# Small TensorE products as 64- and 32-wide array tiles in an HGRN2 attention and low-rank mixer kernel

## The chip, the cores and the metric

The kernel runs on one core of one Trainium2 chip. The core's engines each work through their own instruction stream: TensorE (PE, with its weight loads listed as PEld), VectorE (DVE), ScalarE (ACT), GpSimd (POOL) and SyncE (SP, which issues DMAs). The metric is the device time of one execution in microseconds; the smaller the better. All operands are 32-bit floats.

## The reference, cut to what matters

Two blocks follow each other. The first is a gated linear recurrence over 768 steps for 4 batches of 8 heads of width 48; the second a mixer over the 768 positions (rank 32) and the 384 channels.

```python
# attention: q, k, v, f_logit are (4, 8, 768, 48)
f = sigmoid(f_logit)
for t in range(S):
    state = f[:, :, t, :, None] * state + k[:, :, t] (x) v[:, :, t]   # 48 x 48 per head
    y[:, :, t] = q[:, :, t] @ state
x = y as (4, 768, 8 * 48)
# mixer: U (768, 32), V (32, 768), w_ch1 (384, 1536), w_ch2 (1536, 384)
h = x.transpose(0, 2, 1) @ U @ V
u = x + h.transpose(0, 2, 1)
out = u + relu(u @ w_ch1) @ w_ch2
```

## The kernel before, in words

**Units.** A unit is a pair of heads of one batch; there are 16, four for each batch. The two heads (`par` 0 and 1) lie on partitions 0 to 47 and 64 to 111 of the transposed tiles (`PAD` is 64), and the 768 steps are cut into `NCH` = 6 chunks of `C` = 128. `prepare(n)` makes what unit n needs: VectorE turns f, k and q (`turned`, L237), ScalarE takes the sigmoid (L255), VectorE scans the gates from the back and from the front (L261, L280), and GpSimd multiplies k and q by the scans (L276, L285). `keep` also makes `whole`, the product of the gates of each chunk.

**`attend(n)`** has five pieces. `scores(0)` and `scores(1)` multiply k and q of each head and chunk (L308, `sc`; 48 rows, at partition 0 or 64) and VectorE masks the result into `A` (L315). `kept` transposes five chunks of k, both heads at once, on TensorE (L325, `pt`), and ScalarE copies them to `kb` (L329). `states` multiplies `kb` with v for both heads at once (L334, `ds`, 128 x 96), so that half of every product belongs to the wrong head; VectorE masks that half away with `own` (L339, `dn`), GpSimd scales by `whole` (L345, `st`), and four VectorE steps carry the state from chunk to chunk (L349). `read` adds, chunk by chunk, q times the state before the chunk (L359) and `A` times v for each head (L362) into `y`, and ScalarE copies y into `x` (L367).

**The mixer** of a batch is a list of pieces (`mixer_pieces`): `low_rank` (L73, `ph`: six products of 128 rows and 32 columns of U into one sum of 32 partitions, copied to `h` at L76), `mix` (L80, `pu`: 32 rows of V and h; VectorE adds to x at L81), `turn` (L89, `put`: transposes, ScalarE copy L91), `ch1` (L96, `pz`, ReLU at L99) and `ch2` (L105, `po`, add at L108, then the DMA out).

**Order.** The loop at L388 runs the pieces of `attend(n)`, puts the pieces of `prepare(n + 1)` between them, and after each calls `fill`, which takes pieces from the list `todo`. While batch 0's units run, `todo` holds the weight loads (L24: each weight is a 64-bit float in memory, DMA into `w_raw`, six VectorE steps L46 to L53, two GpSimd steps L54 and L55); while later units run, it holds the mixer of the batch before. The mixer of batch 3 runs alone at the end. Each engine's order within that is set by the tile framework's scheduler, which is why pieces interleave. PSUM has three double-bank tiles for sc, pt and y (`ps_big`) and two single-bank tiles for all else (`ps_mm`).

A TensorE product of 32-bit floats is seen in the trace as two MATMUL records, each with its own LDWEIGHTS record; a transpose is seen as one.

Of the kernel before, what the change touches and what calls it, by code (L numbers as in the profile page):

```python
# [16 lines left out]
WP = 384  # L17
# [6 lines left out]
def weight_loader(nc, pool, one, dma):  # L24
# [7 lines left out]
    def load(dst, w):  # L32
        if w.dtype == F32:
            dma.dma_start(out=dst, in_=w)
            return
        rows, cols = dst.shape
        raw = pool.tile([P, WP], U64, name="w_raw")
        dma.dma_start(out=raw[0:rows, 0:cols], in_=w)
# [21 lines left out]
def mixer_pieces(nc, b, x, U, V, w1, w2, ident, out, two, three, zp, ps_mm):  # L60
# [3 lines left out]
    R, FF = U.shape[2], w1.shape[2]  # L64
    NDC, NFC = DM // P, FF // P
# [4 lines left out]
    def low_rank():  # L70
        pm = ps_mm.tile([P, 512], F32, name="ph", tag="mm")
        for c in range(NCH):
            nc.tensor.matmul(pm[0:R, 0:DM], lhsT=U[:, c, :], rhs=x[:, c, :],  # L73
                             start=(c == 0), stop=(c == NCH - 1))
        h[0] = two.tile([R, DM], F32, name="h")
        nc.scalar.copy(h[0], pm[0:R, 0:DM])  # L76
# [46 lines left out]
def factored_path(ctx, tc, q, k, v, f_logit, moe_U, moe_V, moe_w_ch1, moe_w_ch2, out, ok):  # L123
# [20 lines left out]
    PW = 2 * D  # L144

    assert S % (2 * C) == 0 and H % 2 == 0 and NB < D <= PAD and PAD == 2 * NB and S % NB == 0
    assert DM % P == 0 and FF % P == 0 and FF % WP == 0 and DM == WP and DM <= 512 and R <= P
    assert G * PW <= 512 and G * C <= 512 and (NCH - 1) * PW <= 512

# [50 lines left out]

    own = const.tile([P, PW], F32, name="own")
    nc.vector.memset(own, 0.0)
    for par in range(2):
        for lo, n in ((0, NB), (NB, D - NB)):
            nc.vector.memset(own[par * PAD + lo : par * PAD + lo + n, par * D : (par + 1) * D], 1.0)
# [13 lines left out]
    V = const.tile([R, S], F32, name="V")  # L219
    load = weight_loader(nc, two, one, nc.sync)  # L220
    weights = [lambda c=c: load(U[:, c, :], moe_U[c * P : (c + 1) * P, :]) for c in range(NCH)]
    weights += [lambda o=o: load(V[:, o : o + WP], moe_V[:, o : o + WP]) for o in range(0, S, WP)]
# [70 lines left out]
    def attend(n):  # L293
# [28 lines left out]
        def kept():  # L322
            pt = ps_big.tile([P, 2, 512], F32, name="pt", tag="big")
            for c in range(NCH - 1):
                nc.tensor.transpose(pt[:, c // G, (c % G) * C : (c % G + 1) * C], T["k"][:, chunk[c]], ident)  # L325
            kb = T["kb"] = two.tile([P, NCH - 1, C], F32, name="kb")
            for a in range(2):
                lo, hi = a * G, min((a + 1) * G, NCH - 1)
                nc.scalar.copy(kb[:, lo:hi, :].rearrange("p c d -> p (c d)"), pt[:, a, 0 : (hi - lo) * C])  # L329

        def states():
            ds = ps_mm.tile([P, 512], F32, name="ds", tag="mm")
            for c in range(NCH - 1):
                nc.tensor.matmul(  # L334
                    ds[:, c * PW : (c + 1) * PW], lhsT=T["kb"][:, c, :],
# [406 lines left out]
```

## Time and profile before

| | |
|---|---|
| median of the runs | 722.86 us (lowest 721.62) |
| profiled execution | 721.53 us, of which 719.6 us span |
| PE busy | 614.4 us (85%), 2489 MATMUL records |
| PEld busy | 403.6 us (56%) |
| DVE busy | 336.6 us (47%) |
| POOL busy | 143.5 us (20%) |
| ACT busy | 98.1 us (14%) |
| mean granted TensorE clock | 0.913 |

Busy PE time is modelled from the records and is not useful work at full speed; a record's start is measured, so the distance from one start to the next is the better price. Idle time of an engine that nobody waits for costs nothing. The granted clock takes two values in this trace, 1.00 and 0.50 of full speed, and the mean over a stretch tells how much of it ran at the lower one.

### The profile page before, as it was taken

The numbers are of one execution on the slowest core, as the hardware profiler recorded it, in microseconds if no ns is written. First come the engines' busy times: TensorE is split into PE (matmuls) and PEld (weight loads), VectorE is DVE, ScalarE is ACT, GpSimd is POOL, SyncE is SP. The second block draws the span as 40 slices with busy tenths as digits, with TensorE's granted clock in tenths as the row PEclk, the third lists the DMA queues.
The fourth block names the chain that finished last, engine by engine and source line by source line (L and its number), as shares of the span: only waits on it lengthen the run. The fifth ranks groups of instructions, "written<-read, shape, count | busy, mean of one in ns | idle before, by whom it ended". The sixth has DMA issues, their size and how long they took to land.

```text
span 719.6 us, 6593 instructions
## 1 busy us (share of the span) xinstructions
PE 614.4 (85%) x2489; PEld 403.6 (56%) x2489; DVE 336.6 (47%) x539; ACT 98.1 (14%) x205; POOL 143.5 (20%) x123
## 2 busy tenths in 40 slices
PE   0776248297199999989999999999999999999996
PEld 0765244074176666547665766576656664555553
DVE  6668798999984566254553542354211201000000
ACT  1100001012021031011320120112201200220210
POOL 3123374656632220102111111012100000000000
PEclk9999999559589999975999999859999999799999
DMA  9801354533497320452202522100000000000000
GB/s 205 155 1 31 97 122 109 142 109 120 136 215 145 85 52 20 108 117 50 64 16 71 140 58 70 53 8 10 0 23 11 1 12 23 0 1 22 12 12 26
DMA packets 42176, 47.71 MB, mean 66 GB/s; under 512 B 29783, under 2 KB 32855, under 8 KB 42135
## 3 DMA queue, kind: packets, MB, share of 16 engines
q1 hardware_dynamic: 42134, 47.20, 27.2%
q8 instruction: 21, 0.34, 0.2%
q14 instruction: 21, 0.16, 0.1%
HBM read 42.47 MB, written 4.72 MB: 66 GB/s over the span
## 4 chain that ended last, share of the span: by engine, by line
PE 76%; DVE 14%; DMA 3%; issue 3%; POOL 2%; ACT 1%; SPq 1%; DVEq 0%; ACTq 0%; POOLq 0%
PE pz L96 25%; PE po L105 25%; PE sc L308 5%; PE y L362 5%; PE ds L334 4%; PE y L359 3%; PE pu L80 3%; PE ph L73 2%; DMA w_raw<-in_moe_w_ch_dram 2%; DVE kT L237 2%; PE put L89 2%; PE pt L325 2%; DVE w_m L48 2%; DVE X L261 1%; DVE fT L237 1%
## 5 line engine op out<-in xcount | busy, mean ns | idle before, releaser
L96 PE MATMUL pz<-uT,w 128*128 128x384 f32 x576 | 200.9, 502 | 0.0
L105 PE MATMUL po<-w,z 128*128 128x384 f32 x576 | 188.7, 487 | 0.0
L105 PEld LDWEIGHTS po<-w,z 128*128 128x128 f32 x576 | 108.7, 190 | 74.3
L96 PEld LDWEIGHTS pz<-uT,w 128*128 128x128 f32 x576 | 109.6, 196 | 71.2 <-issue 5.5
L308 PE MATMUL sc<-qT,kT 48*128 48x128 f32 x384 | 45.9, 370 | 86.9 <-POOL qT L285 86.9
L108 DVE TENSOR_TENSOR o<-x,po 128x384 f32<-128x384 f32 x24 | 13.3, 554 | 181.5 <-PE po L105 181.5
L308 PEld LDWEIGHTS sc<-qT,kT 48*128 48x128 f32 x384 | 35.5, 252 | 105.2 <-POOL qT L285 89.2
L99 ACT ACTIVATE z<-pz 128x384 f32<-128x384 f32 x96 | 47.1, 490 | 228.2 <-PE pz L96 228.2
L362 PE MATMUL y<-v_nat,A 128*128 128x48 f32 x384 | 70.7, 318 | 0.0
L362 PEld LDWEIGHTS y<-v_nat,A 128*128 128x128 f32 x384 | 69.2, 251 | 2.4
L276 POOL TENSOR_TENSOR kT<-kT,X 128x768 f32<-128x768 f32 x16 | 30.3, 1894 | 200.0 <-DVE kT L237 187.9
L315 DVE TENSOR_TENSOR A<-sc,causal 128x384 f32<-128x384 f32 x64 | 33.2, 551 | 63.6 <-PE sc L308 63.5
L359 PE MATMUL y<-st,qT 128*128 128x96 f32 x160 | 42.9, 359 | 4.8 <-POOL st L345 4.8
L237 DVE STREAM_TRANSPOSE qT<-q_raw 128x768 f32<-128x768 f32 x16 | 33.5, 2094 | 18.7 <-PE y L359 18.7
L285 POOL TENSOR_TENSOR qT<-qT,Y 128x768 f32<-128x768 f32 x16 | 29.4, 1839 | 63.2 <-DVE qT L237 62.8
L54 POOL TENSOR_SCALAR w_m<-w_m 128x384 f32<-128x384 f32 (+2 forms) x32 | 34.4, 1074 | 36.4 <-DVE w_m L48 23.4
L261 DVE TENSOR_TENSOR_SCAN X<-fz,ends 128x768 f32<-128x768 f32 x16 | 28.1, 1757 | 26.0 <-ACT fz L255 20.4
L345 POOL TENSOR_TENSOR st<-dn,whole 128x480 f32<-128x480 f32 x16 | 16.5, 1033 | 111.6 <-DVE dn L339 110.2
L359 PEld LDWEIGHTS y<-st,qT 128*128 128x128 f32 x160 | 32.7, 251 | 7.2 <-POOL st L345 5.9
L237 DVE STREAM_TRANSPOSE fT<-f_raw 128x768 f32<-128x768 f32 x16 | 33.3, 2079 | 6.4 <-DMA f_raw<-in_f_logit_dram 4.4
L237 DVE STREAM_TRANSPOSE kT<-k_raw 128x768 f32<-128x768 f32 x16 | 33.2, 2074 | 0.0
L80 PE MATMUL pu<-h,V 32*128 32x384 f32 x48 | 30.1, 731 | 3.1 <-ACT uT L91 1.7
(52 smaller groups left out, 424.0 us busy)
## 6 DMA issues: line engine op xcount, KB each, us to landing
w_raw<-in_moe_w_ch_dram SPq DMA_DIRECT2D x24, 384.0 KB, 3.6
f_raw<-in_f_logit_dram SPq DMA_DIRECT2D x63, 142.0 KB, 3.6
k_raw<-in_k_dram SPq DMA_DIRECT2D x63, 142.0 KB, 4.4
q_raw<-in_q_dram SPq DMA_DIRECT2D x63, 142.0 KB, 4.1
v_nat<-in_v_dram SPq DMA_DIRECT2D x32, 144.0 KB, 5.2
out_dram<-o SPq DMA_DIRECT2D x24, 192.0 KB, 1.9
w_raw<-in_moe_U_dram SPq DMA_DIRECT2D x6, 32.0 KB, 3.2
w_raw<-in_moe_V_dram SPq DMA_DIRECT2D x2, 96.0 KB
```

What stands on the lines that cost most here:

```text
L54: nc.gpsimd.tensor_scalar(m, m, 2.0**-20, None, ALU.mult)
L80: nc.tensor.matmul(pm[:, 0:DM], lhsT=V[:, t * P : (t + 1) * P], rhs=h[0], start=True, stop=True)
L96: nc.tensor.matmul(pm[:, 0:HALF], lhsT=w1[:, m, i * P : (i + 1) * P], rhs=uT[a][:, m, :], start=(m == 0), stop=(m == NDC - 1))
L99: nc.scalar.activation(z[a, i], pm[:, 0:HALF], AF.Relu)
L105: nc.tensor.matmul(pm[:, 0:DM], lhsT=z[a, i][:, s * P : (s + 1) * P], rhs=w2[:, i, :], start=(i == 0), stop=(i == NFC - 1))
L237: nc.vector.transpose(t.rearrange("p (i c) -> p c i", c=TB), bass.AP(src_tile.tensor, src_tile.offset, [list(src_tile.ap[0]), [D, TB], [1, ...
L261: nc.vector.tensor_tensor_scan(backwards(X, S - 1, S), backwards(f, S, S), backwards(ends, S - 1, S), 0.0, ALU.mult, ALU.add,)
L276: nc.gpsimd.tensor_tensor(kT, kT, T["X"], ALU.mult)
L308: nc.tensor.matmul(sc[:, par, c * C : (c + 1) * C], lhsT=T["k"][rows[par], chunk[g * G + c]], rhs=T["q"][rows[par], chunk[g * G + c]], sta ...
L315: nc.vector.tensor_tensor(T["A"][:, par, g * G : (g + 1) * G, :], sc[:, par, 0 : G * C].rearrange("p (c i) -> p c i", i=C), causal.unsquee ...
L359: nc.tensor.matmul(o, lhsT=T["q"][:, chunk[c]], rhs=T["st"][:, c - 1, :], start=True, stop=False, skip_group_check=True)
L362: nc.tensor.matmul(o[:, par * D : (par + 1) * D], lhsT=T["A"][:, par, c, :], rhs=vt[:, c, par, :], start=(c == 0), stop=True, skip_group_c ...
```

## The change

Small TensorE products get a smaller part of the array each, at different partitions, next to each other:

- **Score and state parts of y** (`read`). The 128 steps of a chunk are cut into two halves of 64 (`HC`), which land on PSUM partitions 0 to 63 and 64 to 127. The state part is now four products a chunk (48 rows, 64 columns, 48 wide: two heads by two halves), all 20 ahead of the score part; the score part is four products a chunk (128 rows, 64 columns, 48 wide), 24 in all. Each head has its own bank of `y`.
- **State updates** (`states`). Ten products of 128 rows, 64 columns, 48 wide, one per head, each on its own 64 partitions. The wrong-head half does not arise, so `own`, `dn` and the GpSimd step go: one VectorE step scales from PSUM into `st` (240 wide), and the four carry steps are 48 wide.
- **Transposes of k** (`kept`). Ten of 64 rows instead of five of 128, one bank per head; one ScalarE copy of 640 in place of two of 384 and 256.
- **U product** (`low_rank`). The six products go to four 32-column tiles (`NG` = 4), so that `h` is four partial sums on 128 partitions; V is loaded four times, one copy below the other, so that `mix` has 128 rows and adds the four sums up.

The lines of the changed kernel are shifted: `ph` L79, `pu` L86, `put` L95, `pz` L102, `po` L111, `pt` L327, `ds` L335, `st` L341 and L346, `y` L363 (state) and L372 (score).

```diff
     def load(dst, w, copies=1):
+        rows, cols = dst.shape
+        n = rows // copies
...
-        dma.dma_start(out=raw[0:rows, 0:cols], in_=w)
+        for i in range(copies):
+            dma.dma_start(out=raw[i * n : (i + 1) * n, 0:cols], in_=w)
...
         for c in range(NCH):
-            nc.tensor.matmul(pm[0:R, 0:DM], lhsT=U[:, c, :], rhs=x[:, c, :],
-                             start=(c == 0), stop=(c == NCH - 1))
-        h[0] = two.tile([R, DM], F32, name="h")
-        nc.scalar.copy(h[0], pm[0:R, 0:DM])
+            g = slice((c % NG) * R, (c % NG + 1) * R)
+            nc.tensor.matmul(pm[g, 0:DM], lhsT=U[:, c, :], rhs=x[:, c, :],
+                             start=(c < NG), stop=(c >= NCH - NG))
+        h[0] = two.tile([P, DM], F32, name="h")
+        nc.scalar.copy(h[0], pm[:, 0:DM])
...
-    V = const.tile([R, S], F32, name="V")
+    V = const.tile([P, S], F32, name="V")
...
             for c in range(NCH - 1):
-                nc.tensor.transpose(pt[:, c // G, (c % G) * C : (c % G + 1) * C], T["k"][:, chunk[c]], ident)
...
+                for par in range(2):
+                    r = slice(par * PAD, (par + 1) * PAD)
+                    nc.tensor.transpose(pt[:, par, c * PAD : (c + 1) * PAD], T["k"][r, chunk[c]], ident[r, r])
+            kb = T["kb"] = two.tile([P, 2, NCH - 1, PAD], F32, name="kb")
+            nc.scalar.copy(kb.rearrange("p h c d -> p h (c d)"), pt[:, :, 0 : (NCH - 1) * PAD])
...
-                nc.tensor.matmul(
-                    ds[:, c * PW : (c + 1) * PW], lhsT=T["kb"][:, c, :],
-                    rhs=vt[:, c].rearrange("p h d -> p (h d)"), start=True, stop=True,
-                )
-            dn = two.tile([P, NCH - 1, PW], F32, name="dn")
...
-            nc.gpsimd.tensor_tensor(
-                st, dn, T["whole"][:, 1:NCH].unsqueeze(2).broadcast_to((P, NCH - 1, PW)), ALU.mult
+                for par in range(2):
+                    nc.tensor.matmul(
+                        ds[par * PAD : (par + 1) * PAD, c * D : (c + 1) * D],
+                        lhsT=T["kb"][:, par, c, :], rhs=vt[:, c, par, :], start=True, stop=True,
+                    )
+            st = T["st"] = two.tile([P, NCH - 1, D], F32, name="st")
             nc.vector.tensor_tensor(
+                st, ds[:, 0 : (NCH - 1) * D].rearrange("p (c e) -> p c e", e=D),
+                T["whole"][:, 1:NCH].unsqueeze(2).broadcast_to((P, NCH - 1, D)), ALU.mult,
             )
...
+            for c in range(1, NCH):
+                for par in range(2):
+                    for a in range(2):
+                        nc.tensor.matmul(
+                            o(a, par, c),
+                            lhsT=T["q"][rows[par], c * C + a * HC : c * C + (a + 1) * HC],
+                            rhs=T["st"][rows[par], c - 1, :],
+                            start=(c == 1), stop=False, skip_group_check=True,
+                        )
             for c in range(NCH):
...
                 for par in range(2):
+                    for a in range(2):
+                        nc.tensor.matmul(
+                            o(a, par, c), lhsT=T["A"][:, par, c, halves[a]], rhs=vt[:, c, par, :],
+                            start=False, stop=True, skip_group_check=True,
+                        )
```

What stands on TensorE before, in a unit of batch 1 (`ds`, then `y`, with products of the mixer of batch 0 between them; x6 counts products):

```order
L96 MATMUL pz<-uT,w_127 128x384 x6
L334 MATMUL ds<-v_nat,kb 128x96 x5
L96 MATMUL pz<-uT,w_127 128x384 x3
L105 MATMUL po<-w_128,z 128x384 x12
L362 MATMUL y<-v_nat,A 128x48 x2
L359 MATMUL y<-st,qT 128x96
```

The last two rows go on in turn until `y` has five of L359 and six of L362. At the same place of the changed kernel:

```order
L102 MATMUL pz<-uT,w_121 128x384 x6
L335 MATMUL ds<-v_nat,kb 64x48 x10
L102 MATMUL pz<-uT,w_121 128x384 x3
L111 MATMUL po<-w_122,z 128x384 x12
L363 MATMUL y<-st,qT 64x48 x20
L372 MATMUL y<-v_nat,A 64x48 x24
L111 MATMUL po<-w_122,z 128x384 x24
```

The mixer's products stand where they stood; the 17 products of `y` have become 44, in two blocks, and the state part, which needs `st`, now comes first.

VectorE before, in the first units, from the masks of the scores to the next unit's gates:

```order
L315 TENSOR_TENSOR A<-sc,causal 128x384 x4
L339 TENSOR_TENSOR dn<-ds,own 128x480
L237 STREAM_TRANSPOSE fT<-f_raw_80 128x24x32
L349 SCALAR_TENSOR_TENSOR st<-st,whole 128x96 x3
L261 SCALAR_TENSOR_TENSOR X<-fz_118,ends 128x768
```

and in the changed kernel:

```order
L315 TENSOR_TENSOR A<-sc,causal 128x384 x4
L341 TENSOR_TENSOR st<-ds,whole 128x240
L346 SCALAR_TENSOR_TENSOR st<-st,whole 128x48 x2
L237 STREAM_TRANSPOSE fT<-f_raw_80 128x24x32
L346 SCALAR_TENSOR_TENSOR st<-st,whole 128x48 x2
```

Two of the carry steps now stand ahead of the next unit's turning of f, since they no longer wait for a GpSimd step; the turning of f still stands behind `ds`.

48 lines of the change are left out of this document (16 added, 32 removed).

## The prediction

> **What bounds the kernel now.** I read the page's first two parts, then the chain of waits by engine.
>
> ```profile
> span 719.6 us, 6593 instructions
> PE   0776248297199999989999999999999999999996
> DVE  6668798999984566254553542354211201000000
> PE 76%; DVE 14%; DMA 3%; issue 3%; POOL 2%; ACT 1%; SPq 1%; DVEq 0%; ACTq 0%; POOLq 0%
> ```
>
> Each digit is 18 us. PE has gaps in the first 11 slices (to about 204 us), where batch 0's units run and VectorE also unpacks the weights; from there on it is full. So two stages: a third in which VectorE and the hand-overs decide, and 515 us in which a microsecond of PE is a microsecond of time. I then took windows of that stage; the column PEclk is the granted clock.
>
> ```profile
> core 0: us, PE busy (x) PEld busy (x) DVE busy (x) ACT busy (x) POOL busy (x), PEclk, DMA share, GB/s
> 304.00:308.00 4.00, 4.00 (x23) 1.75 (x24) 3.51 (x4) 0.07 (x1) 0.00 (x0) 1.00 1.25 247
> 316.00:320.00 4.00, 4.00 (x14) 2.00 (x13) 0.95 (x2) 0.48 (x1) 0.00 (x0) 0.50 0.00 0
> 312.00:344.00 32.00, 30.51 (x107) 21.09 (x108) 14.08 (x20) 4.01 (x9) 4.57 (x3) 0.57 0.28 63
> 460.00:492.00 32.00, 32.00 (x120) 22.25 (x119) 15.86 (x24) 5.73 (x13) 4.56 (x3) 0.63 0.06 13
> 608.00:624.00 16.00, 15.73 (x42) 7.57 (x41) 3.10 (x6) 3.50 (x8) 0.00 (x0) 0.68 0.00 0
> ```
>
> Three stretches run partly at half clock, one per batch, each where the mixer's `pu` and `put` pieces stand: 32 x 0.43 / 0.5 = 27.5 us, 23.7 us and 10.2 us, together 61 us. PE is busy all through 316 to 320 and still gets half clock.
>
> Last, the timeline of TensorE for one unit at full clock: start, duration, line, records.
>
> ```profile
> 343.69 0.71 PE L325 MATMUL pt<-ident,kT 128*128 128x128 f32 x5
> 344.23 4.04 PE L96 MATMUL pz<-uT,w 128*128 128x384 f32 x12
> 348.20 0.94 PE L308 MATMUL sc<-qT,kT 48*128 48x128 f32 x12
> 349.07 4.14 PE L96 MATMUL pz<-uT,w 128*128 128x384 f32 x12
> 353.04 1.25 PE L334 MATMUL ds<-v_nat,kb 128*128 128x96 f32 x10
> 354.13 4.06 PE L96 MATMUL pz<-uT,w 128*128 128x384 f32 x12
> 358.03 0.54 PE L362 MATMUL y<-v_nat,A 128*128 128x48 f32 x4
> ...
> 361.76 4.10 PE L96 MATMUL pz<-uT,w 128*128 128x384 f32 x12
> ```
>
> Prices from start to start: `y` 361.76 - 358.03 = 3.73 us for 34 records, 0.110 each; `ds` 1.09 for 10, 0.109 each; `pt` 0.54 for 5. `y` and `ds` cost the same per record though one is mostly 48 and the other 96 wide, so not the width but the weight load of 128 columns sets the slot. `sc`, two heads on rows 0 and 64, does 12 records of the same 128 columns in 0.87, entry and exit included.
>
> **Part by part.** *The slot of a 64-column record.* The weight loads of U (32 columns) and of the mixer (128), both at full clock, and from the chain of waits a run of the mixer's products:
>
> ```profile
> L73 PEld LDWEIGHTS ph<-x,U 128*32 128x32 f32 x12 | 1.2, 109 | 3.2 <-issue 3.2
> L96 PEld LDWEIGHTS pz<-uT,w 128*128 128x128 f32 x7 | 1.3, 190 | 0.9
> ...
> 666.33 23.22 PE pz L96 x72
> ```
>
> 96 columns are 81 ns, 0.84 ns each; 64 columns make the slot 0.11 / 2 = 0.055 us. *Side by side.* If `sc`'s records took turns, 12 would be 1.3 us; 0.87 with entry and exit says that pairs run together: 6 slots of 0.11 are 0.66, which leaves 0.2 us beside the 0.1 us in which the last ones run out. The twelve pz records before `sc` take 0.322 each, as 23.22 / 72 says too, so they are done by 344.23 + 12 x 0.322 = 348.09, 0.11 before `sc`. I price a change between the whole array and a tiled form at 0.15 to 0.2 us.
>
> *y.* State part: 40 records on four tiles, at best 10 slots = 0.55, in pairs 20 = 1.1. Score part: 48 records on two column tiles, 24 slots = 1.32. Three changes of form, 0.5. That is 2.4 to 2.9 against 3.73; I take a gain of 1.1. Two tiles by columns are not seen in the trace: in turn, they would cost 48 slots = 2.64, and y 3.7 to 4.2. *ds.* 20 records in 10 slots 0.55 and two changes 0.35: a gain of 0.2; in turn 1.45, a loss of 0.36. *pt.* Ten records in five paired slots of half the width, 0.3, and two changes: 0.65 to 0.9, a loss of 0.1 to 0.35; I take 0.2, and 0.1 gained at ds. Per unit 1.1 + 0.1 - 0.2 = 1.0 us. In the full stage eight units (6, 7, 9 to 11, 13 to 15) lie outside the slow stretches: **-8 us**.
>
> *U product.* Twelve records one after the other now, in batch 1:
>
> ```profile
> 304.70 4.06 PE L73 MATMUL ph<-x,U 128*32 128x384 f32 x12
> 308.69 0.76 PE L325 MATMUL pt<-ident,kT 128*128 128x128 f32 x5
> ```
>
> 3.99 us, 0.33 a record. In four tiles two rounds of two records, 1.33 and 0.3 of changes: a gain of 2.35; in pairs of tiles 1.6. Batches 1 to 3, on PE's path each time: **-6 us** (5 to 7).
>
> *The clock.* In 304 to 308 stand U's products, 128 rows and 32 columns: clock 1.00. In 316 to 320 stand `pu` with 32 rows, `sc` with 48 and transposes: 0.50, with PE as busy. So rows in use seem to count. With V fourfold, `pu` has 128 rows. At best all 61 us run at full clock and take 30 us less, which also holds the units 8 and 12. But the first stretch begins with a real gap that the change leaves, and `pu` before and after:
>
> ```profile
> 313.49 0.65 PE L89 MATMUL put<-ident,x 128*128 128x128 f32 x3 [2.14 <-DVE x L81]
> 317.93 1.64 PE L80 MATMUL pu<-h,V 32*128 32x384 f32 x2
> 609.03 0.91 PE L80 MATMUL pu<-h,V 32*128 32x384 f32 x2
> ```
>
> (1.64 at half clock, 0.91 at full). At full clock the chain add, turn, copy would show: VectorE's 33 us in these 80 would sit in 50. I take half: **-16 us** (0 to -28).
>
> *The first 204 us.* Unit 1, VectorE with its idle time before, and the PE work it waits for:
>
> ```profile
> 40.18 1.66 PE L308 MATMUL sc<-qT,kT 48*128 48x128 f32 x12 [5.16 <-POOL qT L285]
> 41.77 1.33 PE L325 MATMUL pt<-ident,kT 128*128 128x128 f32 x5
> 44.61 2.45 PE L334 MATMUL ds<-v_nat,kb 128*128 128x96 f32 x10
> ...
> 41.89 1.02 DVE L315 TENSOR_TENSOR A<-sc,causal 128x384 f32<-128x384 f32 x2 [3.64 <-PE sc L308]
> 44.73 1.02 DVE L315 TENSOR_TENSOR A<-sc,causal 128x384 f32<-128x384 f32 x2 [1.82 <-PE sc L308]
> 47.09 0.66 DVE L339 TENSOR_TENSOR dn<-ds,own 128x480 f32<-128x480 f32 x1 [1.34 <-PE ds L334]
> ```
>
> Records here take double. `pt` shares sc's form, so 1.3 becomes 0.7; `ds` 2.45 becomes 1.1 + 0.3. 1.6 us off a chain on which VectorE sits idle, and 0.4 from shorter VectorE steps (dn, of 480, becomes a step of 240): 2 us in each of units 0 to 2. In units 3 to 5 VectorE is full and waits for GpSimd's `st`:
>
> ```profile
> 105.41 1.24 POOL st L345
> L349 DVE SCALAR_TENSOR_TENSOR st<-st,whole 128x96 f32<-128x96 f32 x64 | 23.0, 360 | 10.7 <-POOL st L345 9.4
> L339 DVE TENSOR_TENSOR dn<-ds,own 128x480 f32<-128x480 f32 x16 | 10.5, 655 | 22.3 <-PE ds L334 22.3
> ```
>
> The step goes with its 1.24; that and about 0.3 of VectorE are 1.5 us each. Together 6 + 4.5: **-10 us** (0 if the weights' unpacking holds all, -14). At nothing: one kb copy for two, masks no longer made, four V loads for one on SP (early, in the slices with few DMAs; if they came late, `h` times V at 121 us would wait).
>
> Sum: -8 - 6 - 16 - 10 = -40 from the profiled 721.5, so 681.5; the median stands 1.3 above, and I forecast **682 us** (660 to 700 with the ends above).
>
> **The rivals.** *The clock stays low* (17%): the sum without its 16 is -24, and units 8 and 12 at double price add 4: 721.5 - 28 = 694. For it: nothing shows `pu` with 128 rows. Against: PE was fully busy at 0.50. [...]
>
> *Column tiles take turns* (16%): y 3.7 to 4.2, ds +0.36, pt +0.2, so about +0.9 in eight units, +7; low rank 0; first third -5; the clock -14 of its own. 710, or 724 if the clock stays too. No row shows two column tiles together. [...]
>
> *Every record keeps its slot* (12%, the slower side): each of the 118 records of y, ds and pt holds 0.11 us, as all of y's and ds's do now. y becomes 9.7, ds 2.5, pt 1.4 against 5.4 together, +8.2 a unit: +66 in eight units and +33 in two at half clock, less 20 elsewhere, near 800. From an average of 0.07 us a record (118 x 0.07 + 1.05 = 9.3, +3.9 a unit, 12 unit prices = +47) it eats all gains and 2% more. Against: sc's paired records stand at 0.055.
>
> **How the numbers follow.** Forecast 55%, rivals 17, 16 and 12%. A measurement of this kernel tells about 2% (14 us) from no change: faster is below 708, slower above 737. Forecast and low clock are all faster; of the turns 2 points are faster, 13 the same, 1 slower; the kept slot is slower. Faster 0.74, same 0.13, slower 0.13. The range takes in the forecast's ends, the low clock and the lower half of the turns, 55 + 17 + 8 = 80%: 658 to 714.
>
> **What would show it.** Right: y near 2.6 us between mixer products at full clock, with starts of neighbouring records within a few ns of each other; ph under 2 us; clock 1.00 in the windows of batches 2 and 3 where `pu` stands; PE's gaps before 204 us shorter. Wrong: y's records at even steps of 0.055 or more (turns), of 0.11 (kept slot); 0.50 again at `pu` (clock); VectorE 95% busy and batch 0 still ending at 204 us (no first third). A new wait of y's state block on `st`, which it now needs whole within a microsecond, would cost up to 1 us a unit.

## The result, and the profile after

The changed kernel takes 667.99 us (median of 4 runs, 666.35 to 668.39) against 723.05 of the kernel before (one of its four executions took 947.78 us; without it the median is 722.86): a ratio of 0.924, 95% interval 0.9217 to 0.9264. Its profiled execution took 667.96 us with a span of 666.2, so the span is 53.4 us shorter.

From the page of the changed kernel: the span, the 40 slices (16.7 us each now) of PE and VectorE, and the chain of waits by engine.

```profile
span 666.2 us, 8766 instructions
PE   0555037277099999999999999999999998999996
DVE  5669799999985674365642652473011102000000
PE 67%; DVE 18%; DMA 7%; issue 3%; SPq 2%; POOL 1%; ACT 1%; DVEq 0%; POOLq 0%; ACTq 0%
```

The two stages are still there: gaps in the first 11 slices (to about 183 us), a full PE behind them. The share of VectorE and of DMA on the chain has grown, though the first stage is no larger a part of the whole (its first 183.90 of 666.2 us are 27.6%, before 195.78 of 719.6 us were 27.2%). Why the chain there now runs through other work was not followed. The windows over the three stretches of `pu` and `put`, wide enough to hold every half-clock record of these stretches, with the columns of the prediction's windows (the granted clock stands ahead of the DMA share):

```profile
290.00:350.00 60.00, 57.78 (x413) 35.76 (x414) 35.08 (x49) 14.34 (x30) 7.24 (x4) 0.91 0.30 70
430.00:500.00 70.00, 68.74 (x459) 42.16 (x458) 24.41 (x38) 10.80 (x21) 7.23 (x4) 0.95 0.05 13
550.00:640.00 90.00, 87.43 (x287) 50.62 (x286) 5.87 (x12) 15.11 (x31) 0.00 (x0) 1.00 0.03 11
```

60 x 0.09 / 0.5 = 10.8 us, 70 x 0.05 / 0.5 = 7.0 and none: about 17 us of half clock (10.2 and 6.8 by the clock's own records, less rounded) are left of 61. The three windows are named after the batch whose mixer stands in them; beside the mixer of batch 1 runs unit 8, and beside that of batch 2 unit 12.

Where the 53.4 us come from can be read from marks that both kernels have on TensorE's timeline: the first scores of unit 5 and the U product `ph` of batches 1, 2 and 3. Before (that of batch 1, at 304.70, stands in the prediction; the two rows at 410.15 and 454.50 are the same scores of two neighbouring units at full clock):

```profile
195.78 0.59 PE L308 MATMUL sc<-qT,kT 48*128 48x128 f32 x2 [20.50 <-POOL qT L285]
410.15 0.94 PE L308 MATMUL sc<-qT,kT 48*128 48x128 f32 x12
454.50 0.94 PE L308 MATMUL sc<-qT,kT 48*128 48x128 f32 x12
455.37 4.06 PE L73 MATMUL ph<-x,U 128*32 128x384 f32 x12
602.24 4.03 PE L73 MATMUL ph<-x,U 128*32 128x384 f32 x12 [0.63 <-DVE o L108]
```

and after:

```profile
183.90 1.44 PE L308 MATMUL sc<-qT,kT 48*128 48x128 f32 x10 [21.35 <-POOL qT L285]
287.48 1.48 PE L79 MATMUL ph<-x,U 128*32 128x384 f32 x12
288.90 0.52 PE L327 MATMUL pt<-ident,kT 64*128 64x64 f32 x9
380.53 0.71 PE L308 MATMUL sc<-qT,kT 48*128 48x128 f32 x8
423.45 0.94 PE L308 MATMUL sc<-qT,kT 48*128 48x128 f32 x12
424.32 1.48 PE L79 MATMUL ph<-x,U 128*32 128x384 f32 x12
556.73 1.48 PE L79 MATMUL ph<-x,U 128*32 128x384 f32 x12 [0.63 <-DVE o L114]
```

| stretch, us | before | after | difference |
|---|---|---|---|
| start to first scores of unit 5 | 195.78 | 183.90 | -11.9 |
| to `ph` of batch 1 (units 5 to 7) | 108.92 | 103.58 | -5.3 |
| to `ph` of batch 2 | 150.67 | 136.84 | -13.8 |
| to `ph` of batch 3 | 146.87 | 132.41 | -14.5 |
| to the end | 117.36 | 109.47 | -7.9 |

One unit at full clock goes from 454.50 - 410.15 = 44.35 to 423.45 - 380.53 = 42.92 us: 1.43 less. The U product goes from 3.99 to 288.90 - 287.48 = 1.42: 2.57 less, three times. Taken out of the batch stages (three units and one U product in each of the first two, one U product in the last), that leaves -7.0, -7.6 and -5.3, together -19.9 us, for the mixer stretches with units 8 and 12.

Inside a unit at full clock, the same products as in the prediction's timeline:

```profile
258.08 0.79 PE L335 MATMUL ds<-v_nat,kb 128*64 128x48 f32 x20
258.80 2.20 PE L102 MATMUL pz<-uT,w 128*128 128x384 f32 x6
260.84 7.90 PE L111 MATMUL po<-w,z 128*128 128x384 f32 x24
268.68 0.80 PE L363 MATMUL y<-st,qT 48*64 48x48 f32 x40
269.40 1.61 PE L372 MATMUL y<-v_nat,A 128*64 128x48 f32 x48
270.94 15.75 PE L111 MATMUL po<-w,z 128*128 128x384 f32 x48
```

Start to start: `y` 270.94 - 268.68 = 2.26 us for 88 records (3.73 for 34 before), of which the state part is 0.72 and the score part 1.54; `ds` 0.72 (1.09 before). In the records themselves four of the state part, one for each tile, start at 268.675, .682, .688 and .695, and the next four at 268.768, then four every 0.058 us; the score part starts in pairs 6 to 7 ns apart, a pair every 0.058 us. So neighbours on different tiles run together, weight loads included. The sum of the three parts (`y` -1.47, `ds` -0.37, `pt` 0.54 to 0.46) is -1.92, yet a unit gains 1.43. The rest lies in the full-array products beside the tiled blocks. The first one behind a block starts together with its own weight load (258.802 and 258.801), and the next starts 0.427 us later, the one after that 0.323: the six `pz` records behind `ds` take 2.04 instead of 6 x 0.322 = 1.93. The last one ahead of a block stands 0.416 us ahead of it (268.259 and 268.675): the 24 `po` records ahead of `y` take 7.84 instead of 7.74. Over the unit of the two marks the 114 full-array records take 37.75 us, 37.26 before. Of these 0.49 us about 0.13 stand beside `y`, 0.17 beside `ds` and 0.19 beside `pt`, so that with its neighbours `y` gains 1.34, `ds` gains 0.20 and `pt` loses 0.10.

### The profile page after: what moved, and what is told of

Its sections match the earlier page's. It is cut to its first block, busy times and chain, and to the rows that moved or that the text cites. A ratio compares the mean times of both kernels' runs of the same rounds, so it can differ in the third digit from the quotient of the medians.

```text
span 666.2 us, 8766 instructions
## 1 busy us (share of the span) xinstructions
PE 544.8 (82%) x3593; PEld 339.3 (51%) x3593; DVE 326.5 (49%) x534; ACT 96.8 (15%) x189; POOL 127.3 (19%) x107
## 4 chain that ended last, share of the span: by engine, by line
PE 67%; DVE 18%; DMA 7%; issue 3%; SPq 2%; POOL 1%; ACT 1%; DVEq 0%; POOLq 0%; ACTq 0%
PE po L111 27%; PE pz L102 27%; PE sc L308 4%; PE y L372 3%; DVE w_m L51 2%; DVE kT L237 2%; DMA q_raw<-in_q_dram 2%; PE pu L86 2%; DMA w_raw<-in_moe_w_ch_dram 2%; DMA k_raw<-in_k_dram 2%; DVE fT L237 2%; SPq L179 1%; DVE qT L237 1%; DVE w_head L49 1%; DVE X L261 1%
## 5 line engine op out<-in xcount | busy, mean ns | idle before, releaser
L102 PE MATMUL pz<-uT,w 128*128 128x384 f32 x576 | 202.5, 505 | 1.2 <-ACT z L105 1.2
L111 PE MATMUL po<-w,z 128*128 128x384 f32 x576 | 189.2, 488 | 0.0
L102 PEld LDWEIGHTS pz<-uT,w 128*128 128x128 f32 x576 | 110.0, 196 | 74.4 <-issue 6.3
L111 PEld LDWEIGHTS po<-w,z 128*128 128x128 f32 x576 | 108.7, 190 | 74.7
L308 PE MATMUL sc<-qT,kT 48*128 48x128 f32 x384 | 42.7, 356 | 92.2 <-POOL qT L285 92.2
L57 POOL TENSOR_SCALAR w_m<-w_m 128x384 f32<-128x384 f32 (+1 forms) x32 | 34.1, 1065 | 34.3 <-DVE w_m L51 25.6
L372 PE MATMUL y<-v_nat,A 128*64 128x48 f32 x768 | 32.1, 252 | 0.0
L363 PE MATMUL y<-st,qT 48*64 48x48 f32 x640 | 20.7, 255 | 13.6 <-DVE st L346 8.6
L280 DVE TENSOR_TENSOR_SCAN Y<-fz,starts 128x768 f32<-128x768 f32 x16 | 28.1, 1755 | 6.3 <-POOL qT L285 5.5
L372 PEld LDWEIGHTS y<-v_nat,A 128*64 128x64 f32 x768 | 29.9, 167 | 1.1
L86 PE MATMUL pu<-h,V 128*128 128x384 f32 x48 | 25.0, 622 | 6.1 <-ACT h L82 2.5
L58 POOL TENSOR_TENSOR w<-w_m,w_s 128x384 f32<-128x384 f32 x24 | 26.1, 1087 | 16.1 <-DVE w_s L56 16.0
```

Source lines behind the costliest of these rows:

```text
L57: nc.gpsimd.tensor_scalar(m, m, 2.0**-20, None, ALU.mult)
L86: nc.tensor.matmul(pm[:, 0:DM], lhsT=V[:, t * P : (t + 1) * P], rhs=h[0], start=True, stop=True)
L102: nc.tensor.matmul(pm[:, 0:HALF], lhsT=w1[:, m, i * P : (i + 1) * P], rhs=uT[a][:, m, :], start=(m == 0), stop=(m == NDC - 1))
L111: nc.tensor.matmul(pm[:, 0:DM], lhsT=z[a, i][:, s * P : (s + 1) * P], rhs=w2[:, i, :], start=(i == 0), stop=(i == NFC - 1))
L308: nc.tensor.matmul(sc[:, par, c * C : (c + 1) * C], lhsT=T["k"][rows[par], chunk[g * G + c]], rhs=T["q"][rows[par], chunk[g * G + c]], sta ...
L372: nc.tensor.matmul(o(a, par, c), lhsT=T["A"][:, par, c, halves[a]], rhs=vt[:, c, par, :], start=False, stop=True, skip_group_check=True,)
```

## The experiments

Each kernel is a part of the change alone, the change with one part undone, or one thing in another order. Ratios are to the kernel before with their 95% intervals; half clock is worked out as above, from the windows of each run.

### The attention parts alone, and the low-rank part alone

The first kernel has the changed `pt`, `ds`, `st` and `y` with the low-rank part as before; the second is the kernel before with these lines:

```diff
+            g = slice((c % NG) * R, (c % NG + 1) * R)
+            nc.tensor.matmul(pm[g, 0:DM], lhsT=U[:, c, :], rhs=x[:, c, :],
+                             start=(c < NG), stop=(c >= NCH - NG))
+        h[0] = two.tile([P, DM], F32, name="h")
...
+    V = const.tile([P, S], F32, name="V")
...
+    weights += [lambda o=o: load(V[:, o : o + WP], moe_V[:, o : o + WP], P // R) for o in range(0, S, WP)]
```

> The attention part of the change alone (y, ds, pt as tiles, no mask and GpSimd step); U product, h and V as before, with 32 rows in pu. Theory (tiles side by side, clock set by rows in use): y about 2.26, ds 0.72, pt 0.46 us at full clock as in the whole change, so 1.9 us in eight full-clock units (-15), -14 up to unit 5 and its y, and units 8 and 12 at double price (-8): about 685 us, with the half clock still near 55 to 61 us around pu. Rival (the clock rose because the attention parts became shorter and denser, not because of pu's rows): half clock down to some 17 us here too, and 672 to 678 us.

> The U product in four tiles and V fourfold alone; the attention part as before. Theory: ph 1.4 instead of 4.0 us three times (-8), and with 128 rows in pu most of the 61 us at half clock goes (-14 to -20): 693 to 700 us, half clock 10 to 25 us after batch 0. Rival (clock by how busy PE is, whatever the rows): half clock stays near 60 us and the time is 713 to 716.

Attention parts alone: 685.06 us, 0.9488 (0.945 to 0.9526). Low-rank part alone: 702.83 us, 0.9722 (0.9703 to 0.9741). Their spans are 36.4 and 19.5 us shorter than before; 55.9 together, against 53.4 for both at once, so they hardly touch each other. The timeline (two neighbouring units) and the window of batch 2 with the attention parts alone:

```profile
382.57 0.60 PE L306 MATMUL sc<-qT,kT 48*128 48x128 f32 x6
425.50 0.72 PE L306 MATMUL sc<-qT,kT 48*128 48x128 f32 x8
```

```profile
430.00:500.00 70.00, 69.89 (x446) 42.01 (x444) 24.02 (x37) 12.44 (x24) 7.22 (x4) 0.85 0.04 9
```

A unit takes the same 42.93 us as in the changed kernel, so the unit's gain is the attention parts' own. The half clock stays: 70 x 0.15 / 0.5 = 21 us in batch 2, and by the other two windows 20 in batch 1 (0.83) and 14 in batch 3 (0.92), 56 in all. The clock belongs to the low-rank part: with it alone 21 us are left.

The low-rank part gave less than expected, for two reasons. Its U product of batch 1 starts at 306.5, 1.8 us later than before: VectorE waits for the loads of V, which take four turns on SP, and then 2.05 us for the weights queued behind them; before, it has neither wait there. (No run gives V its four loads alone.)

```profile
85.56 0.38 DVE L49 TENSOR_SCALAR w_head<-w_raw 128x384 uint32<-128x384 uint32 x1 [0.98 <-DMA w_raw<-in_moe_V_dram]
```

And beside the U product's 7.7 us, 41 us less half clock brought 13.6 us, 0.33 us for each and not 0.5.

### What the clock counts: rows named, data, changes of form

Three kernels with everything as before except that `h` and V have 128 rows. In the first, U's columns stand four times in the weights of an untiled `ph` (so `h` has four equal copies) and V is loaded four times at a quarter of its size. In the second, U's added columns are zero, so 96 of the rows of `h` are zeros. The third is the first with a small product of 32 rows ahead of each `pu`.

```diff
-            nc.tensor.matmul(pm[0:R, 0:DM], lhsT=U[:, c, :], rhs=x[:, c, :],
+            nc.tensor.matmul(pm[:, 0:DM], lhsT=U[:, c, :], rhs=x[:, c, :],
...
+        nc.scalar.copy(U[:, c, :].rearrange("p (g r) -> p g r", r=R),
+                       U1[:, c, :].unsqueeze(1).broadcast_to((P, P // R, R)))
```

In the second the copy fills only U's own columns of a zeroed tile, and V keeps its size; the third adds two lines to the first:

```diff
+        nc.scalar.copy(U[:, c, 0:R], U1[:, c, :])
...
+        nc.tensor.matmul(pm[:, DM : DM + 8], lhsT=V[0:R, t * P : (t + 1) * P], rhs=h[0][0:R, 0:8],
+                         start=True, stop=True)
```

> The kernel before with U's 32 columns repeated four times in the weights of ph (128 columns, no tiles, six products one after the other) and V fourfold at a quarter, so that pu has 128 rows and nothing is tiled that was not; the computation is the same. Theory (rows in use set the clock): ph stays at 4.0 us, half clock after batch 0 falls from 61 to 10 to 30 us, time 701 to 709. Rival (clock by busy time): half clock stays near 60 us and the time within 2 us of before, 720 to 724.

> As the run with U's columns repeated, but the 96 added columns of U are zero, so that pu has 128 rows in its instruction while 96 rows of h stream zeros; the computation is the same. Theory a (rows named by the instruction count): half clock after batch 0 as in that run, 20 to 35 us, time 707 to 713. Theory b (what counts is how much of the array works on data that is not zero): half clock near 60 us, 720 to 724.

> As the run with U's columns repeated, plus, ahead of each of the 24 pu products, one of 32 rows and 8 wide into unused columns of the same PSUM tile (extra work, not used): pu keeps 128 rows, but the array changes its form on both sides of it as in the kernel before. Theory (rows set the clock): half clock after batch 0 stays at 20 to 35 us; the extra products cost 0.3 to 0.5 us each, 18 of them on the path: 714 to 720 us. Rival (it was the drained changes of form around pu, not its rows, that held the clock down): half clock back to 50 to 62 us and 724 to 732 us.

Measured: 710.27 us, 0.9806 (0.9772 to 0.9841); with zeros 708.99, 0.981 (0.9783 to 0.9837); with the small products 713.38, 0.9899 (0.9865 to 0.9933). The windows of batches 1 and 2 before, and then in the first,

```profile
290.00:350.00 60.00, 57.86 (x215) 36.15 (x214) 21.68 (x31) 9.04 (x20) 6.38 (x4) 0.77 0.45 102
430.00:500.00 70.00, 70.00 (x280) 45.19 (x279) 28.77 (x39) 9.41 (x20) 7.07 (x5) 0.83 0.13 36
```

```profile
290.00:350.00 60.00, 55.98 (x227) 36.32 (x227) 24.58 (x31) 9.77 (x21) 8.06 (x5) 0.86 0.44 102
430.00:500.00 70.00, 68.09 (x301) 44.89 (x299) 29.97 (x44) 10.43 (x23) 9.16 (x6) 0.93 0.13 36
```

With zeros they read the same 0.86 and 0.93, with PE busy for 55.97 and 68.08 us. With the small products, batch 1:

```profile
290.00:350.00 60.00, 58.38 (x243) 37.87 (x243) 26.43 (x37) 10.26 (x22) 7.88 (x5) 0.89 0.45 102
```

Over the three batches the half clock is 27, 27 and 23 us, against 61 before. The time of the first kernel lies 1.3 us above the range expected, that of the third 0.6 below; the other is inside. From `ph` of batch 1 on the first kernel is 12.5 us faster (its span is 10.4 shorter, and that `ph` comes 2.1 later), 0.37 us for each of the 34 us: PE's idle time in the three windows grows from 3.6 to 8.5 us, which is about what lacks to half of 34. Naming 128 rows in `pu` takes more than half of it away, with no tiled product in the kernel; that 96 rows hold zeros makes no difference, and an extra change of form ahead of each `pu` doesn't bring it back. Busy time doesn't order these windows. A record at half clock lasts longer (two of `pu` 1.64 us before, 0.91 at full clock) and so adds to the busy time itself, which leaves batch 1 open; but in batch 2 PE was busy for all of the 70 us before and had 0.83, and with 128 rows it stands idle for 1.9 us and has 0.93. A clock that goes by busy time alone, the rival of the first run, does not fit these two rows of batch 2; what differs between the two kernels is the rows that `pu` names, with the products and loads that give it these rows.

### Whether the order of tiles matters

The score part's 24 products in another order: all of one column tile, then all of the other.

```diff
-            for c in range(NCH):
-                for par in range(2):
-                    for a in range(2):
+            for a in range(2):
+                for c in range(NCH):
+                    for par in range(2):
```

> The whole change with the 24 score products of y in another order: all 12 of the first half of the steps (one column tile), then all 12 of the other, same instructions. Theory (neighbours overlap only where they use different tiles): the score part takes 48 slots of 0.058 instead of 24, +1.4 us a unit at full clock, and the time is 680 to 686 us. Rival (the shorter weight load alone is the gain, or the engine pairs them from further away): 667 to 669.

681.12 us, 0.941 (0.9359 to 0.946). The score part at full clock:

```profile
272.82 2.81 PE L372 MATMUL y<-v_nat,A 128*64 128x48 f32 x48
275.55 15.75 PE L111 MATMUL po<-w,z 128*128 128x384 f32 x48
```

2.73 us instead of 1.54, for the same 48 records: 0.057 each, one after the other. About thirteen of the change's 55 us hang on neighbours being on different tiles: 1.19 us in each of the eleven units from unit 5 on, and 3.4 us more of half clock in batch 2 (0.93 for 0.95). The four runs spread more than the others', from 677.73 to 684.90.

### What a change of form costs

State and score products in turn, chunk by chunk, which makes eleven blocks of the two:

```diff
-            for c in range(1, NCH):
-                for par in range(2):
-                    for a in range(2):
...
             for c in range(NCH):
+                if c:
+                    for par in range(2):
+                        for a in range(2):
...
                 for par in range(2):
                     for a in range(2):
                         nc.tensor.matmul(
                             o(a, par, c), lhsT=T["A"][:, par, c, halves[a]], rhs=vt[:, c, par, :],
-                            start=False, stop=True, skip_group_check=True,
+                            start=(c == 0), stop=True, skip_group_check=True,
```

> The whole change with y's 44 products chunk by chunk, score part and state part in turn as in the kernel before, same products: 11 blocks in place of 2. Theory (each change of the array's form costs 0.15 to 0.2 us): nine more changes, +1.3 to +1.8 us a unit in the eleven units on PE's path, 680 to 688 us. Rival (a change costs only where the weight load is 128 columns wide, or hides behind the other tiles): 666 to 670.

674.86 us, 0.9333 (0.9291 to 0.9376): faster than expected. The blocks at half way through a `y`:

```profile
331.04 0.33 PE L364 MATMUL y<-st,qT 48*64 48x48 f32 x8
331.30 0.44 PE L372 MATMUL y<-v_nat,A 128*64 128x48 f32 x8
331.67 0.33 PE L364 MATMUL y<-st,qT 48*64 48x48 f32 x8
```

A pair of blocks takes 0.63 us from start to start, where the slots (two of the state part, four of the score part) would be 0.116 + 0.23 = 0.35: two changes cost 0.28, 0.14 each. Over the whole `y`, 3.7 us against 2.26 is 1.46 for nine more changes, 0.16 each. So the price was as taken; the miss is that the 10 us of half clock of batch 1 are gone in this kernel (1.00 over 290 to 350 us). That was not part of any theory, and the next runs follow it.

### State part or score part first

```diff
+            for c in range(NCH):
+                for par in range(2):
+                    for a in range(2):
+                        nc.tensor.matmul(
+                            o(a, par, c), lhsT=T["A"][:, par, c, halves[a]], rhs=vt[:, c, par, :],
+                            start=(c == 0), stop=(c == 0), skip_group_check=True,
+                        )
             for c in range(1, NCH):
...
-                            start=(c == 1), stop=False, skip_group_check=True,
-                        )
-            for c in range(NCH):
...
                             start=False, stop=True, skip_group_check=True,
```

> The whole change with y's score part ahead of the state part, so that the state part no longer stands waiting for the carry steps. Theory (the waits of 0.5 and 0.7 us in units 8 and 12 and some of the half clock there are lost time): 663 to 667 us. Rival (what is gained there is lost to pieces of the mixer that the scheduler puts between the blocks, each with a change of form): 667 to 671.

659.22 us, 0.912 (0.91 to 0.9141): 8.8 us faster than the changed kernel, 3.8 below the range expected, and the fastest kernel here. Nearly all of it lies in the stages of batches 1 and 2 (130.62 for 136.84, 129.97 for 132.41), and the half clock falls from 17 to 3 us. In the changed kernel, the `y` of unit 8 on TensorE's timeline (in the window of batch 1), and the scores of unit 9 behind it:

```profile
301.22 0.33 PE L363 MATMUL y<-st,qT 48*64 48x48 f32 x8 [0.48 <-DVE st L346]
...
303.22 0.64 PE L363 MATMUL y<-st,qT 48*64 48x48 f32 x16 [0.74 <-DVE st L346]
...
304.46 2.80 PE L372 MATMUL y<-v_nat,A 128*64 128x48 f32 x48
...
307.60 1.65 PE L308 MATMUL sc<-qT,kT 48*128 48x128 f32 x10
```

and with the score part first (the last row is of the `y` of unit 12, in the window of batch 2):

```profile
301.81 1.09 PE L370 MATMUL y<-st,qT 48*64 48x48 f32 x40
...
303.64 0.94 PE L308 MATMUL sc<-qT,kT 48*128 48x128 f32 x12
...
431.92 0.94 PE L370 MATMUL y<-st,qT 48*64 48x48 f32 x24 [1.40 <-DVE st L346]
```

In the changed kernel TensorE waits for `st` twice among products of 48 rows and transposes, and from 304.0 to 314.2 the clock's records have 0.50 and what stands there takes nearly double (the score part 2.80 for 1.61, the scores 1.65 for 0.94). With the score part first `st` is ready when the state part comes, and the scores that follow take 0.94. In batch 2 it waits 1.40 us even so, and there the 3 us of half clock stand.

### The step from GpSimd, and the transposes of k

First the scaling of the state updates given back to GpSimd (VectorE copies `ds`, GpSimd scales it); then the transposes of k as before, 128 by 128, with `ds` taking its halves from them; then these old transposes together with the score part first.

```diff
-            nc.vector.tensor_tensor(
-                st, ds[:, 0 : (NCH - 1) * D].rearrange("p (c e) -> p c e", e=D),
+            dn = two.tile([P, NCH - 1, D], F32, name="dn")
+            nc.vector.tensor_copy(dn, ds[:, 0 : (NCH - 1) * D].rearrange("p (c e) -> p c e", e=D))
+            nc.gpsimd.tensor_tensor(
+                st, dn, T["whole"][:, 1:NCH].unsqueeze(2).broadcast_to((P, NCH - 1, D)), ALU.mult
```

```diff
-                    nc.tensor.transpose(pt[:, par, c * PAD : (c + 1) * PAD], T["k"][r, chunk[c]], ident[r, r])
+                nc.tensor.transpose(pt[:, c // G, (c % G) * C : (c % G + 1) * C], T["k"][:, chunk[c]], ident)
...
-                        lhsT=T["kb"][:, par, c, :], rhs=vt[:, c, par, :], start=True, stop=True,
+                        lhsT=T["kb"][:, c, par * PAD : (par + 1) * PAD], rhs=vt[:, c, par, :], start=True, stop=True,
```

> The whole change, but the state is copied by VectorE and scaled by GpSimd as before (240 wide). Theory (in the first units the hand-over to GpSimd is on the path): the step of about 0.6 us and its hand-over, with VectorE held up beside it, cost 0.6 to 1.3 us in each of six units: 671 to 676 us. Rival (what the first third gained came from TensorE's shorter chain alone): 667 to 669.

> The whole change with the transposes of k as before: five of 128 rows on the whole array, two copies. Theory: 0.1 us a unit at full clock (+1), and in the first units, at half clock, pt 1.3 instead of 0.5 us and two changes of form more between the score blocks (+0.5 to +1 in five units): 671 to 675 us. Rival (transposes are hidden or equal in price): 667 to 669.

> Score part of y first, and the transposes of k as in the kernel before. Theory (pt as tiles is worth about 3 us in the first third and 1 us later; what the run with the old transposes gained came from half-clock windows that happened to fall away, and the score-first order has hardly any of these): 661 to 664 us, 2 to 5 more than score-first alone. Rival (old transposes are the better choice): 654 to 658 us.

GpSimd's step back: 670.53 us, 0.9267 (0.924 to 0.9294). That is 2.5 us more than the changed kernel, and the two intervals overlap; the first scores of unit 5 come at 185.96 instead of 183.90, so what the step is worth lies in the first third, if it is more than noise; this run doesn't settle it. The old transposes: 666.1 us, 0.9203 (0.9174 to 0.9232), not the 671 to 675 expected. The first third is slower as expected (186.98 for 183.90), but again the half clock of batch 1 is gone (1.00 over 290 to 350 us), while batch 2 has 10 us of it instead of 7. With the score part first, the old transposes cost 8.8 us, more than either theory had: 668.06, 0.925 (0.9226 to 0.9274), and there half clock of batch 1 is back (7 us). The `y` of unit 8 with the old transposes,

```profile
306.62 0.94 PE L363 MATMUL y<-st,qT 48*64 48x48 f32 x24 [0.17 <-DVE st L346]
```

and with both:

```profile
306.56 0.64 PE L370 MATMUL y<-st,qT 48*64 48x48 f32 x16 [1.67 <-DVE st L346]
...
308.51 1.65 PE L308 MATMUL sc<-qT,kT 48*128 48x128 f32 x12
```

So the half clock of these kernels goes by how long the `y` of unit 8 or 12, beside a mixer's `pu` and `put`, waits for `st`: 0.17 us, none; 1.67 us, half clock. The same holds wherever it can be looked up: in the eight kernels with tiled `y` and a tiled U product there are sixteen such places (units 8 and 12). In eleven of them the `y` waits 1.0 to 1.7 us for `st`, and the granted clock of the windows used here is 0.91 to 0.98; in five it waits 0 to 0.17 us, and the clock is 1.00. (The last experiment below is one of the eight.) In the low-rank part alone, with the old `y`, 10 us of half clock also follow a wait for `st`, of 1.89 us at 322.12. Idle time alone is not it: in the changed kernel PE waits 1.30 us ahead of `pu` at 290.72, and with the old transposes it is idle for 2.5 of the 60 us of batch 1, and the clock stays at 1.00. Nor does half clock need such a wait where `pu` has 32 rows: before, PE was never idle over batch 2 and had 24 us of it.

VectorE's rows of the changed kernel show where the wait is from:

```profile
298.73 0.41 DVE L341 TENSOR_TENSOR st<-ds,whole 128x240 f32<-128x240 f32 x1 [0.18 <-PE ds L335]
299.06 2.07 DVE L237 STREAM_TRANSPOSE kT<-k_raw 128x768 f32<-128x768 f32 x1
300.92 0.24 DVE L346 SCALAR_TENSOR_TENSOR st<-st,whole 128x48 f32<-128x48 f32 x1
...
301.49 2.29 DVE L346 SCALAR_TENSOR_TENSOR st<-st,whole 128x48 f32<-128x48 f32 x3
```

The 2.07 us turn of a next unit's k stands between the scaling of `st` and its carry steps, and it seems to cost a second time: GpSimd's product of that k follows it, from 301.30 to 303.10, and beside that product the carry step at 301.49 lasts 1.68 us, where the two behind it last 0.27 each. With the score part first the turn stands ahead of the scaling in batch 1 (297.47), and between the two in batch 2 (the last three carry steps last 2.29 us there too), where the 1.40 us are.

### The wait for st taken away

The changed kernel, state part first, with the state updates ahead of the second half of the scores; in units 8 and 12 VectorE's turn of k then stands behind the carry steps.

```diff
-        return [lambda: scores(0), kept, lambda: scores(1), states, read]
+        return [lambda: scores(0), kept, states, lambda: scores(1), read]
```

> The changed kernel with one line in another order: the state updates of a unit are issued ahead of the second half of its scores instead of behind it; every unit does the same work, and the state part of y still comes ahead of its score part. In the changed kernel VectorE's 2.07 us turn of the next k stands between the scaling of st and its carry steps in the first unit of batches 1 and 2; here it stands behind them. In those two places TensorE waited 0.48 + 0.74 and 0.49 + 0.74 us for st, and 10 and 7 us of half clock follow. So far the half clock has appeared behind such a wait in every profile that has one and in none that has not. Theory, the waits for st among few-row products bring the half clock: it falls from 17 us to 0 to 4, the waits go, 657 to 662 us. Rival, the 48-row products of the state part bring it by themselves, wherever st is ready: half clock 14 to 20 us, only the 2.4 us of waits go, 664 to 667 us. Second rival, the scores of the second half now come late and y waits for their masks instead: as slow as the changed kernel, 666 to 670 us, with a wait of y on A in place of that on st.

662.58 us, 0.9168 (0.9152 to 0.9184). The score part of the `y` of unit 8, and the windows:

```profile
307.42 1.61 PE L372 MATMUL y<-v_nat,A 128*64 128x48 f32 x48
```

```profile
290.00:350.00 60.00, 59.87 (x462) 36.72 (x461) 37.23 (x52) 14.91 (x30) 7.29 (x4) 1.00 0.42 94
430.00:500.00 70.00, 70.00 (x487) 43.09 (x486) 26.32 (x43) 11.23 (x22) 8.78 (x4) 1.00 0.05 15
```

No wait for `st` in units 8 and 12, and no half clock in the windows: 0 for 17 us, with the same products of 48 rows in the same block. That rules out the first rival, and no wait of `y` on its masks has come. The stages of batches 1 and 2 take 128.09 and 127.99 us, 8.8 and 4.4 less than in the changed kernel; PE's idle time in the two windows falls from 3.5 to 0.1 us, and 17 us of half clock are worth at most 8.5, which leaves 1.3 us of the 13.2 without a name. What no theory had: up to `ph` of batch 1 it is 7.7 us slower. The first scores of unit 5 come 3.9 us later (187.81), and `ph` of batch 1 at 295.13 instead of 287.48. So the whole gains 5.4 us, and the time is half a microsecond above the range expected. The first `put` of all waits 5.50 us for VectorE's add to x (at 116.45), 0.82 in the changed kernel (at 111.74); whether this is what makes that stretch slower was not tested, and a kernel that issues the updates early only from batch 1 on was not tried. The order of the scores moved together with the wait, so strictly this run shows the two together; the sixteen places, where the wait came and went with five different edits, point to the wait.

## Why the prediction was right

The forecast of 682 us was 14 us too high; the direction and every term's sign were right, and each term of the sum was taken too small, the eight units and the clock most of all.

| term | forecast | measured |
|---|---|---|
| eight units at full clock | -8 | -11.4 (8 x 1.43); -13.9 by the marks, with unit 5 |
| U product, three times | -6 | -7.7 |
| mixer stretches, clock | -16 | -19.9 |
| first third | -10 | -11.9 |

*What bounds the kernel.* Holds: behind the first third, what TensorE no longer does is no longer in the time.

*The slot of a 64-column record.* Taken as 0.055 us, measured 0.058. The loads of the score part last 138 ns each, more than two slots, and one starts on each tile every 0.058 us, so the loads overlap on one tile too; the price measured is the step from load to load, not their length.

*y.* The step that was mis-sized: 2.4 to 2.9 us with 2.63 taken, and 2.26 measured. The score part came as reckoned with entry and exit (24 slots, 1.54), and the state part near the better end, four tiles at a time (10 slots of 0.058 and 0.14 of change make the 0.72). *ds* 0.72 instead of about 1.0. *pt* 0.46 instead of 0.74. Changes between two tiled forms, priced at 0.15 to 0.2, cost 0.14 to 0.16; those to and from the full array, priced inside the blocks, lie half beside them, about 0.1 us ahead and 0.1 behind. With these neighbours `y` gains 1.34 for 1.1, `ds` 0.20 for 0.1, and `pt` loses 0.10 for 0.2.

*U product.* Two rounds in four tiles and 0.3 of changes were 1.64; it takes 1.42, changes included.

*The clock.* The reason named holds: the low-rank part alone left 21 of the 61 us, and 128 rows in `pu` without tiles took 34 of the 44 us. Half of the 30 us was taken because the chain add, turn, copy would show. In fact 44 of 61 us went, worth 0.33 to 0.37 us each where the low-rank or row change stood alone. The prediction's reason for the rest does not hold: the gap at the start of the first stretch, 2.14 us ahead of `put`, which the change was to leave, is 0.15 us now (1.30 us stand ahead of `pu`, at clock 1.00). What goes with the last 17 us are the waits for `st`. So of the signs named, a clock of 1.00 came in batch 3 but not in batch 2 (0.95), where it takes the last experiment, which orders the waits away.

*The first third.* -10 forecast, -11.9 measured, but not by its terms. From first scores to first scores, units 0 to 4 gain 1.6, 1.7, 4.6, 2.7 and 1.2 us, where 2 were forecast for units 0 to 2 and 1.5 for 3 to 5; that the total is near is in part luck. Taking GpSimd out, the reason for the 1.5, is worth 2 us by the run that gave the step back (185.96 for 183.90), if it is more than noise. The four loads of V, costed at nothing, take 1.8 us up to `ph` of batch 1 in the low-rank part alone (306.52 for 304.70). That is the one step of the sum that was wrong in kind: cover was named for it, and it was not there.

*The rivals.* The clock stays low: the window of batch 3 at 1.00 says no. Column tiles take turns: records do when neighbours share a tile (0.057 us each) and do not as the change orders them (48 records in 24 slots of 0.058 us). Every record keeps its slot: 0.026 us a record in `y` as a whole.

*What would show it.* The new wait of `y` on `st` was named, at up to 1 us a unit. It is 2.4 us in all behind 200 us; more of its price lay in the 17 us of half clock that came with it, and the two orders that take it away, in both batches or in batch 1, are worth 5 and 9 us.

## What to carry to other kernels

Put small products on the array so that neighbours lie on different tiles, and keep products of one form together: here the order of tiles alone was about 13 us and a change of form 0.15 us. A product with few rows may cost more than its time: here 128 rows in `pu` in place of 32 took 34 of 61 us of half clock away, and the last 17 went with the waits for `st` among products of 48 rows. Try rows that such a product does not need, and see that nothing among such products waits. When a tiled block needs an input late in another engine's queue, start with the part that does not need it; look at the timeline afterwards, since this order was worth 8.8 us here, and with the old transposes nothing (668.06 for 666.10).

## What was not expected of the hardware

- With 128 rows in `pu` half clock fell from 61 to 27 us, whether 96 of them held data or zeros, while a PE that was never idle over batch 2, with 32 rows in `pu`, had 0.83 against 0.93.
- Waits of 1.0 to 1.7 us among few-row products came with half clock in eleven places of eleven, and waits of 0 to 0.17 us in none of five; a wait of 1.30 us ahead of products of 128 rows did not. What the clock goes by is not shown beyond these places.
- The half-clock stretches differ by even steps: 10.24 and 6.83 us in the clock's records of the changed kernel, and 27.31, 23.89 and 10.24 us in the three batches before. The difference of the first two is 3.41 us; the five are three, two, eight, seven and three times that. Why is not shown.
- A microsecond of half clock was worth 0.33 to 0.37 us, not 0.5, where PE's idle time grew in its place (from 3.6 to 8.5 us in the three windows with 128 rows in `pu`).
- The mean granted clock of a run misleads. The first 100 us of the changed kernel, and of the one with the score part first:

```profile
0.00:100.00 100.00, 34.31 (x504) 31.09 (x504) 76.00 (x146) 9.63 (x16) 35.36 (x42) 1.00 0.54 119
```

```profile
0.00:100.00 100.00, 33.07 (x560) 30.74 (x560) 75.63 (x146) 9.50 (x16) 35.68 (x42) 0.71 0.55 119
```

PE is nearly as busy in both and the first twelve records of scores of units 0 and 1 take 1.65 us in both, as at half clock; yet one stretch reads 1.00 and the other 0.71, and the mean over the span is lower in the faster kernel (0.895 against 0.969). The first clock record of the changed kernel stands at 150.4 us, and ahead of it the clock reads as full (1.00 in each window of 20 us up to 160). Windows behind the first third can be compared, these means can't.
